# Loading v of later batches from GpSimd's queue, and spreading its block sums as one row

## The chip, the cores and the metric

The kernel runs on one core of a Trainium2 chip. The core has a matrix engine (TensorE, PE in the profile; its weight loads are PEld), a vector engine (VectorE, DVE), a scalar engine (ScalarE, ACT), GpSimd (POOL) and SyncE (SP). Each runs its own list of instructions in order and waits on semaphores. Transfers between memory and the on-chip buffers are issued from SP or from GpSimd, each with a queue of its own, and both queues are worked off by the same 16 DMA engines.

The metric is the time of one execution on the device, in microseconds, and it is judged against the kernel before.

## The reference

Four batches of 768 positions, 8 heads of 64, all fp32. For every batch an attention with a short window and with block summaries, then a gate that chooses one expert of eight for the whole batch, and that expert's two-layer network:

```python
k_sum = k.reshape(B, H, nb, block, D).max(axis=3)      # block = 32, nb = 24
v_sum = v.reshape(B, H, nb, block, D).mean(axis=3)
mask_l = np.abs(pos[:, None] - pos[None, :]) < window  # window = 16
scores_s = scale * einsum(q, k_sum) + np.log(block)
a = softmax(concat([where(mask_l, scale * q @ k.T, -1e9), scores_s]))
attn = a @ concat([v, v_sum])
...
pooled = x.mean(axis=1)                                # x: attn, heads side by side, 768 x 512
logits = pooled @ w_gate
e = argmax(logits);  gate_w = softmax(logits)[e]
out = gate_w * (relu(x @ w1[e]) @ w2[e])               # w1[e] 512 x 1024, w2[e] 1024 x 512
```

The output is 4 x 768 x 512 in fp32. Which expert's weights are loaded is known only when the attention of that batch is done.

## The kernel before

**The work of one batch.** q and k are loaded with a cast to bf16 by GpSimd's queue (`load_qk`, L197), in halves of four heads. For each of four pairs of heads TensorE transposes k and q (`tk` L403, `tq` L427), VectorE (in batch 0 ScalarE) copies k out into windows of 96 positions (`ek`, L425/L423), takes the block maxima (`km`, L445), and ScalarE spreads them (`kb`, L455). Two halves per pair follow: scores (`qk`, L463), exponential on ScalarE (L474), mask on VectorE (L478), the product with v (`av`, L496, called AV below), normalisation on VectorE (`nm`, L509 and L510), and once per pair the transpose of the result (`tx` L520, `xc` L528).

v is loaded in fp32 from SP's queue, one issue per head, with rows of 64 elements, that is 256 bytes (`load_v`, L209), into the one buffer `v_f`. VectorE casts it in four steps of two heads into `vblk` (L295), of which there are two that alternate by batch. `halo_v` (L297) copies the overlap of the windows from partition to partition. Then `v_ops` (L326) makes the block sums: `vs` multiplies with the 0/1 matrix `bind` (L355), `ev` copies the sums out (L367, `vsb`), and `bc` (L372) spreads them by DMA into rows 96 to 119 of `vblk`, once for each of the 12 query blocks. AV reads those rows, so it waits for `bc`.

The gate (`gate`, L625): logits on TensorE (L633), the maximum and its index on VectorE (L643 to L648), then GpSimd reads the index into a register and issues the loads of w1 and w2 of that expert with a cast to bf16 (L664, L670). The expert's network (`moe`, L712, "MoE 0" to "MoE 3" below): first layer L725 with ReLU on ScalarE (L740), second layer L759 with scaling (L769), and stores on SP (L772). The weights have two buffers, as have q and k.

**What sets the order.** The code that looks like a program only adds operations with an engine, an estimated duration, dependencies and "after" (issue order alone) to a planner, `Sched` (L22). At the end `run` (L67) plays these estimates through, engine by engine, prefers what has the longest tail of work behind it, and emits the instructions in that order. So each engine's list is fixed when the kernel is built. A transfer's end is estimated in L120 to L125: it starts 0.8 us after its issue or when its queue is free, takes `dma`, is lengthened by what the other queue still has to do (up to its own length), and is seen 1.2 us later. Where a transfer comes later than planned, everything behind the waiting instruction in that engine's list waits too.

The accumulator tile `ops` in PSUM has one buffer that `vs`, AV and the gate share in the order in which they are added. The loop at L794 adds attention of batch b, the gate of b, `v_ops` of b+1 and the MoE of b; so the block sums of b+1 come after the gate of b.

**The order of the loads before.** On GpSimd's queue: q and k of batch 0, first half of q and k of batch 1 (L801), w(0), second half of batch 1 (L817), first half of batch 2, w(1), second half of batch 2, first half of batch 3, w(2), second half of batch 3, w(3). On SP's queue, beside these: v(0), v(1), then v(2) after w(0) has been issued and the sums of batch 1 have left (`vl`, L807), then v(3) likewise.

Of the kernel before, what the change touches and what calls it, by code (L numbers as in the profile page):

```python
# [21 lines left out]
class Sched:  # L22
# [3 lines left out]
    URGENT = 3.0  # L26

# [39 lines left out]
    def run(self, t0):  # L67
# [28 lines left out]
        for _ in self.ops:  # L96
# [38 lines left out]
def kernel(  # L135
# [16 lines left out]
    QB = 64  # L152
# [38 lines left out]
    ]  # L191
    kts = [const_pool.tile([128, NJ, 128], BF16, name=f"kT{i}") for i in range(3)]
# [16 lines left out]
    def load_v(b, h):  # L209
        if b > 0:  # L210
            nc.sync.dma_start(v_f[16:80, :, h, :], v[b, h].rearrange("(j p) d -> p j d", p=QB))  # L211
            return
# [113 lines left out]
    def v_ops(b, loads):  # L326
# [17 lines left out]
        for gs in groups:  # L344
# [4 lines left out]
            st = {}  # L349

            def vs(b=b, gs=gs, st=st):
                ps = ops_pool.tile([128, 512], FP32, name="ops")
                for j in range(NJ):
                    for i, hg in enumerate(gs):
                        nc.tensor.matmul(  # L355
                            ps[32 * i : 32 * i + 32, 0 : HW * (D + 1)],
                            lhsT=bind[:, j, :],
                            rhs=vblks[b % 2][0:80, j, hg * HW : (hg + 1) * HW, :],
                            start=(j == 0),
                            stop=(j == NJ - 1),  # L360
                        )
                st["ps"] = ps

            def ev(b=b, gs=gs, st=st):
                n = 32 * len(gs)
                st["sb"] = sm_pool.tile([64, HW, D + 1], BF16, name="vsb")
                nc.vector.tensor_copy(  # L367
                    st["sb"][0:n],
                    st["ps"][0:n, 0 : HW * (D + 1)].rearrange("p (h c) -> p h c", c=D + 1),
                )  # L370

            def bc(b=b, gs=gs, st=st):  # L372
                for i, hg in enumerate(gs):
                    nc.sync.dma_start(
                        vblks[b % 2][KW:NR, :, hg * HW : (hg + 1) * HW, :],
                        st["sb"][32 * i : 32 * i + NB].unsqueeze(1).to_broadcast([NB, NJ, HW, D + 1]),
                    )
# [247 lines left out]
    def gate(b, x_ops, w_deps):  # L625
# [72 lines left out]
        o_ld = add("POOL", 1.5, [o_mx] + w_deps, ldf)  # L698
# [92 lines left out]
    casts, bcs = v_ops(0, v_loads)  # L791
    moe_last = {}
    w_order = []
    for b in range(B):  # L794
# [3 lines left out]
        sch.prio = 0.0  # L798
# [12 lines left out]
        sequence()  # L811
        w = gate(b, x_ops, moe_last.get(b - 2, []))
        w_order = [w[2]]
        sch.prio = 0.0
        if nxt < B:
            casts, bcs = v_ops(nxt, vl)
            qk_loads[nxt, 2] = qk_loads[nxt, 3] = add(  # L817
                "POOL", 1.3, prev, lambda n=nxt: load_qk(n, 4, 8), dma=4.7,
                after=[w[2], qk_loads[nxt, 0]],
            )  # L820
# [34 lines left out]
```

## Time and profile before

| | us |
|---|---|
| median of 3 runs | 229.79 (228.34 to 229.96) |
| the profiled execution's own time | 229.69 |
| its span in the profile | 228.1 |
| PE busy | 163.5 (72%) |
| VectorE busy | 100.9 (44%) |
| ScalarE busy | 96.9 (42%) |
| GpSimd busy | 24.6 (11%) |
| GpSimd's queue, packets' share of the 16 DMA engines | 13264 packets, 14.68 MB, 40.3% |
| SP's queue, likewise | 33584 packets, 15.47 MB, 32.2% |

The terms of the prediction are made against 229.69, the execution whose rows are read; it is 0.1 under the median, and 1.6 of it lie around the span.

How the views are read. The first page cuts the span into 40 slices of 5.7 us; a digit is the busy share in tenths. PEclk is TensorE's granted clock in tenths of full speed. A row in the order of time has the start, the duration, engine and line, operation, what it writes and reads, how many, and in brackets the idle time of that engine before it with what ended it. A row of the waits names who waited for whom, with the total, the number and the longest. The chain of waits starts from the last instruction and goes back, at each step, to what released it. The stretches give the busy time of each engine, the granted clock, the DMA engines' busy share (over 1 where packets of two queues overlap) and GB/s. "SPq" is the issuing of transfers on SP; a long SPq row is an issue that was held up.

### The profile page before, as it was taken

To read this page: it belongs to the slowest core of one execution; us is meant where nothing else is said; L and a number is where in the kernel's file an instruction comes from. 1 tells how busy PE (TensorE), PEld (TensorE's weight loads), DVE (VectorE), ACT (ScalarE), POOL (GpSimd) and SP (SyncE) were. 2 spreads that over 40 slices of the span, in tenths; PEclk is the share of its full clock that TensorE was granted. 3 is DMA by queue.
4 is the path that set the end of the run, shared out by engine and by line. 5 is a ranking of instruction groups with operands and counts; after the bars stand their busy time and mean duration, and the time that the engine had idled before them with its cause. 6 is when DMAs were issued, how large, how long until landed. Compare 5 with 4: busy or idle time off the path is not lost.

```text
span 228.1 us, 4604 instructions
## 1 busy us (share of the span) xinstructions
PE 163.5 (72%) x1938; PEld 97.3 (43%) x1960; DVE 100.9 (44%) x207; ACT 96.9 (42%) x182; POOL 24.6 (11%) x43
## 2 busy tenths in 40 slices
PE   0266797478770598993890588994998999089992
PEld 0244675354440465551450455542455544045540
DVE  5364788961302978740302969501269611000000
ACT  2121675334431265553140266623467954025532
POOL 7226000340000000240000000220000002000000
PEclk9999999999995559998598579999799999659998
DMA  6999994299999604399999703199970016990033
GB/s 105 206 183 166 213 174 84 32 165 171 207 197 192 80 3 73 89 156 222 200 196 179 204 0 67 50 166 237 252 139 3 3 50 151 251 194 3 0 152 124
DMA packets 46870, 30.45 MB, mean 133 GB/s; under 512 B 28225, under 2 KB 42145, under 8 KB 46753
## 3 DMA queue, kind: packets, MB, share of 16 engines
q0 software_dynamic: 13264, 14.68, 40.3%
q1 hardware_dynamic: 33584, 15.47, 32.2%
q8 instruction: 15, 0.25, 0.5%
q14 instruction: 7, 0.05, 0.1%
HBM read 36.06 MB, written 6.29 MB: 186 GB/s over the span
## 4 chain that ended last, share of the span: by engine, by line
PE 36%; DMA 28%; SPq 15%; DVE 10%; ACT 5%; issue 3%; POOL 1%; POOLq 1%; ACTq 0%; DVEq 0%
DMA v_f<-in_v_dram 15%; PE hps L725 11%; DMA q_nat<-in_q_dram 9%; SPq L211 9%; PE hps L759 8%; DMA w_sb<-in_moe_w_dram 5%; SPq L214 4%; PE ops L355 3%; PE tps L520 3%; PE tps L431 3%; DVE kT L425 3%; PE kps L406 3%; DVE vblk L295 2%; PE sc L463 2%; PE ops L496 2%
## 5 line engine op out<-in xcount | busy, mean ns | idle before, releaser
L725 PE MATMUL hps<-xT_b,w_sb 128*128 128x256 bf16 (+1 forms) x242 | 55.2, 371 | 14.3 <-DMA w_sb<-in_moe_w_dram 12.6
L740 ACT ACTIVATE hT_sb<-hps 128x512 bf16<-128x512 f32 (+1 forms) x64 | 29.8, 489 | 38.2 <-PE hps L725 36.8
L759 PE MATMUL hps<-w_sb,hT_sb 128*128 128x512 bf16 x184 | 43.2, 380 | 0.6 <-issue 0.3
L725 PEld LDWEIGHTS <-w_sb 128*128 128x128 bf16 x256 | 24.7, 108 | 30.3 <-DMA w_sb<-in_moe_w_dram 12.5
L474 ACT ACTIVATE aT<-sc 128x768 bf16<-128x768 f32 x32 | 25.9, 809 | 14.9 <-PE sc L463 14.6
L406 PE MATMUL kps<-identb,k_nat 96*64 96x96 bf16 x256 | 11.3, 249 | 25.5 <-DVE kT L425 18.0
L478 DVE TENSOR_TENSOR aT<-aT,mask 120x768 bf16<-120x768 bf16 x32 | 17.7, 556 | 23.0 <-ACT aT L474 22.9
L295 DVE CAST vblk<-v_f 80x1536 bf16<-80x1536 f32 x16 | 15.2, 956 | 26.4 <-DMA v_f<-in_v_dram 26.4
L759 PEld LDWEIGHTS <-hT_sb 128*128 128x128 bf16 x192 | 17.8, 98 | 19.8 <-issue 0.2
L769 ACT ACTIVATE o_sb<-hps,gcol 128x512 f32<-128x512 f32 x24 | 16.5, 686 | 22.4 <-PE hps L759 15.4
L528 ACT ACTIVATE xT_b<-tps 128x768 bf16<-128x768 bf16 x16 | 13.0, 810 | 27.4 <-PE tps L520 27.4
L406 PEld LDWEIGHTS <-k_nat 96*64 96x64 bf16 x256 | 9.4, 139 | 28.0 <-issue 20.6
L664 POOL DMA_DIRECT2D w_sb<-in_moe_w_dram x5 | 3.8, 757 | 156.9 <-DVE grec L684 116.8
L496 PE MATMUL ops<-vblk,aT 120*64 120x65 bf16 x384 | 14.4, 220 | 7.2 <-DMA vblk<-vsb 4.1
L510 DVE TENSOR_TENSOR xs<-ops,rv 128x384 bf16<-128x384 f32 x32 | 17.8, 557 | 1.1
L496 PEld LDWEIGHTS <-aT 120*64 120x64 bf16 x384 | 10.8, 130 | 16.4 <-DVE xs L510 4.7
L425 DVE COPY kT<-kps 128x1152 bf16<-128x1152 bf16 x12 | 16.1, 1346 | 0.5 <-PE kps L406 0.5
L463 PE MATMUL sc<-qT,kT 64*128 64x64 bf16 x384 | 13.8, 215 | 3.0 <-ACT aT L474 1.6
L445 DVE TENSOR_REDUCE kmx<-kT 128x24 bf16<-128x768 bf16 x16 | 15.1, 942 | 0.1
L355 PE MATMUL ops<-vblk,bind 80*32 80x260 bf16 x96 | 11.3, 348 | 5.1 <-DVE vblk L295 5.1
L463 PEld LDWEIGHTS <-kT 64*128 64x128 bf16 x384 | 9.7, 109 | 10.6 <-issue 7.1
L509 DVE RECIPROCAL rv<-ops 128x6 f32<-128x6 f32 x32 | 6.1, 191 | 15.7 <-PE ops L496 15.6
(53 smaller groups left out, 110.6 us busy)
## 6 DMA issues: line engine op xcount, KB each, us to landing
w_sb<-in_moe_w_dram POOLq DMA_DIRECT2D x7, 1024.0 KB, 14.8
out_dram<-o_sb SPq DMA_DIRECT2D x24, 256.0 KB, 2.0
v_f<-in_v_dram SPq DMA_DIRECT2D x24, 192.0 KB, 8.5
k_nat<-in_k_dram POOLq DMA_DIRECT2D x6, 384.0 KB, 19.4
q_nat<-in_q_dram POOLq DMA_DIRECT2D x6, 384.0 KB, 20.9
v_f<-in_v_dram SPq DMA_DIRECT2D x7, 240.0 KB, 6.7
vblk<-vsb SPq DMA_DIRECT2D x8, 146.2 KB
vblk<-vblk SPq DMA_DIRECT2D x6, 178.8 KB, 3.8
```

The source lines that it names most:

```text
L211: nc.sync.dma_start(v_f[16:80, :, h, :], v[b, h].rearrange("(j p) d -> p j d", p=QB))
L295: eng.tensor_copy(dst, v_f[:, :, hs, :])
L355: nc.tensor.matmul(ps[32 * i : 32 * i + 32, 0 : HW * (D + 1)], lhsT=bind[:, j, :], rhs=vblks[b % 2][0:80, j, hg * HW : (hg + 1) * HW, :], ...
L406: nc.tensor.transpose(kps[hh * D : (hh + 1) * D, g, 2 : 2 + SP], qk_nat[b][1][:, 2 * pr + hh, g, :], identb[0:SP, 0:SP],)
L425: nc.vector.tensor_copy(kdst, win)
L463: nc.tensor.matmul(sc[:, hh, jj * QB : (jj + 1) * QB], lhsT=sb["kT"][pr][rs, j, :], rhs=sb["qT"][pr][rs, j, :], start=True, stop=True, til ...
L474: nc.scalar.activation(aT, sb["sc"][:, :, 0 : NH * QB], ACT.Exp, scale=SCALE)
L496: nc.tensor.matmul(ops[(j % 2) * QB : (j % 2 + 1) * QB, hh, jj // 2, :], lhsT=aT[0:NR, hh, jj * QB : (jj + 1) * QB], rhs=vb[0:NR, j, 2 * p ...
L510: nc.vector.tensor_tensor(out=sb["xs"][pr][:, hf * NS : (hf + 1) * NS, :, :].rearrange("p s h d -> p h s d"), in0=ops[:, :, :, 0:D], in1=r ...
L725: nc.tensor.matmul(sb["hps"][:, 0 : c1 - c0], lhsT=sb["w1"][:, dt, ft * 128 : (ft + 1) * 128], rhs=sb["xT"][:, dt, c0:c1], start=(dt == 0) ...
L740: nc.scalar.activation(sb["hT"][:, ft, c0:c1], ps["t"][:, 0 : c1 - c0], ACT.Relu)
L759: nc.tensor.matmul(ps["t"], lhsT=sb["hT"][:, ft, st * 128 : (st + 1) * 128], rhs=sb["w2"][:, ft, :], start=(ft == 0), stop=(ft == NFT - 1),)
```

## The change

Five things are changed.

1. `load_v` of batches 1 to 3 issues from GpSimd's queue instead of SP's, still in fp32 and by head.
2. A new function `load_next` adds the loads of one batch as one file: first half of q and k, eight loads of v, second half of q and k. For batch 1 it is called before the gate of batch 0, and the gate's load is ordered after it (`order`). For batch n+1 beyond that it is called when `v_ops` of batch n has been added, ordered after the second weight load of the batch before. So GpSimd's queue holds: batch 0; batch 1; w(0); batch 2; w(1); batch 3; w(2); w(3).
3. The block sums of a later batch are 12 matmuls of 8 heads x 64 columns into one set of 32 partitions, instead of 24 matmuls of 4 heads x 65 columns into two sets. The column of the constant 32, which came out of the matmul, is filled once into two fixed tiles `vsbs`.
4. The spread of a later batch is one issue with rows of 8 heads x 65 bf16 elements, 1040 bytes, instead of two with rows of 520 bytes.
5. The planner's estimates are changed: the lengthening by the other queue is 0.3 of a transfer's own length on GpSimd's queue and up to twice its own length on SP's, and the landing is seen 1.3 us later.

```diff
+    SHARE = {"POOL": 0.3, "SP": 2.0}
...
-                shared = min(op["dma"], max(0.0, other - begin))
+                shared = min(self.SHARE[eng] * op["dma"], max(0.0, other - begin))
                 rings[eng] = begin + op["dma"] + shared
-                op["end"] = rings[eng] + 1.2
+                op["end"] = rings[eng] + 1.3
...
+    vsbs = [const_pool.tile([NB, H, D + 1], BF16, name=f"vsb{i}") for i in range(2)]
...
     def load_v(b, h):
         if b > 0:
-            nc.sync.dma_start(v_f[16:80, :, h, :], v[b, h].rearrange("(j p) d -> p j d", p=QB))
+            nc.gpsimd.dma_start(v_f[16:80, :, h, :], v[b, h].rearrange("(j p) d -> p j d", p=QB))
...
+        for t in vsbs:
+            nc.vector.memset(t[:, :, D : D + 1], float(BLK))
...
                 for j in range(NJ):
-                    for i, hg in enumerate(gs):
-                        nc.tensor.matmul(
-                            ps[32 * i : 32 * i + 32, 0 : HW * (D + 1)],
-                            lhsT=bind[:, j, :],
-                            rhs=vblks[b % 2][0:80, j, hg * HW : (hg + 1) * HW, :],
...
+                    nc.tensor.matmul(
+                        ps[0:32, 0 : n * D],
+                        lhsT=bind[:, j, :],
+                        rhs=vblks[b % 2][0:80, j, hs, 0:D],
...
                 nc.vector.tensor_copy(
-                    st["sb"][0:n],
-                    st["ps"][0:n, 0 : HW * (D + 1)].rearrange("p (h c) -> p h c", c=D + 1),
+                    vsbs[b % 2][:, hs, 0:D],
+                    st["ps"][0:NB, 0 : n * D].rearrange("p (h c) -> p h c", c=D),
                 )
...
-                for i, hg in enumerate(gs):
-                    nc.sync.dma_start(
-                        vblks[b % 2][KW:NR, :, hg * HW : (hg + 1) * HW, :],
-                        st["sb"][32 * i : 32 * i + NB].unsqueeze(1).to_broadcast([NB, NJ, HW, D + 1]),
-                    )
+                nc.sync.dma_start(
+                    vblks[b % 2][KW:NR, :, hs, :],
+                    vsbs[b % 2][:, hs, :].unsqueeze(1).to_broadcast([NB, NJ, n, D + 1]),
+                )
...
-            o_ev = add("DVE", 0.42, [o_vs], ev)
+            o_ev = add("DVE", 0.06 + 0.27 * len(gs), [o_vs, dve_setup] + prev, ev)
...
-            o_bc = add("SP", 0.6 * len(gs), [o_ev], bc, dma=0.8 * len(gs))
+            o_bc = add("SP", 0.5, [o_ev], bc, dma=1.0 * len(gs))
...
-        o_ld = add("POOL", 1.5, [o_mx] + w_deps, ldf)
+        o_ld = add("POOL", 1.5, [o_mx] + w_deps, ldf, after=order)
...
+    def load_next(n, prev, casts, order):
+        sch.prio = 0.0
+        qk_loads[n, 0] = qk_loads[n, 1] = add(
+            "POOL", 1.3, prev, lambda: load_qk(n, 0, 4), dma=4.8, after=order
+        )
+        vl = []
+        for h in range(H):
+            vl.append(
+                add(
+                    "POOL", 0.9, casts, lambda h=h: load_v(n, h), dma=0.95,
+                    after=vl[-1:] or [qk_loads[n, 0]],
+                )
+            )
+        qk_loads[n, 2] = qk_loads[n, 3] = add(
+            "POOL", 1.3, prev, lambda: load_qk(n, 4, 8), dma=4.8, after=vl[-1:]
+        )
+        order_pool[:] = [qk_loads[n, 2]]
+        return vl
...
-        if nxt < B:
-            prev = last_T.get(nxt - 2, [])
-            qk_loads[nxt, 0] = qk_loads[nxt, 1] = add(
-                "POOL", 1.3, prev, lambda n=nxt: load_qk(n, 0, 4), dma=4.7, after=order_pool
-            )
-            vl = []
-            for h in range(H):
-                vl.append(
-                    add("SP", 0.6, casts, lambda n=nxt, h=h: load_v(n, h), dma=0.87, after=vl[-1:] + bcs + w_order)
-                )
...
         sequence()
-        w = gate(b, x_ops, moe_last.get(b - 2, []))
-        w_order = [w[2]]
+        prev = last_T.get(nxt - 2, [])
+        if b == 0:
+            vl = load_next(nxt, prev, casts, order_pool)
+        w = gate(b, x_ops, moe_last.get(b - 2, []), order_pool)
         sch.prio = 0.0
         if nxt < B:
             casts, bcs = v_ops(nxt, vl)
-            qk_loads[nxt, 2] = qk_loads[nxt, 3] = add(
-                "POOL", 1.3, prev, lambda n=nxt: load_qk(n, 4, 8), dma=4.7,
-                after=[w[2], qk_loads[nxt, 0]],
-            )
-            order_pool = [qk_loads[nxt, 2]]
+        if nxt + 1 < B:
+            vl = load_next(nxt + 1, last_T[b], casts, [w[2]])
         moe_last[b] = moe(b, w, xsl)
```

More of the change, by code (lines that the diff above doesn't have):

```diff
@@ L362, in vs, with ev @@
                 st["ps"] = ps
-            def ev(b=b, gs=gs, st=st):
-                n = 32 * len(gs)
-                st["sb"] = sm_pool.tile([64, HW, D + 1], BF16, name="vsb")
+            def ev(b=b, n=n, hs=hs, st=st):
                 nc.vector.tensor_copy(
-                    st["sb"][0:n],
-                    st["ps"][0:n, 0 : HW * (D + 1)].rearrange("p (h c) -> p h c", c=D + 1),
-                )
-            def bc(b=b, gs=gs, st=st):
-                for i, hg in enumerate(gs):
-                    nc.sync.dma_start(
-                        vblks[b % 2][KW:NR, :, hg * HW : (hg + 1) * HW, :],
-                        st["sb"][32 * i : 32 * i + NB].unsqueeze(1).to_broadcast([NB, NJ, HW, D + 1]),
-                    )
+                    vsbs[b % 2][:, hs, 0:D],
+                    st["ps"][0:NB, 0 : n * D].rearrange("p (h c) -> p h c", c=D),
+                )
@@ L623, in attention, with gate @@
         return sequence, xsl, x_ops
-    def gate(b, x_ops, w_deps):
+    def gate(b, x_ops, w_deps, order):
         sb = state[b]
@@ L791 @@
     casts, bcs = v_ops(0, v_loads)
+    def load_next(n, prev, casts, order):
[13 more added lines that the diff above has]
+            "POOL", 1.3, prev, lambda: load_qk(n, 4, 8), dma=4.8, after=vl[-1:]
+        )
+        order_pool[:] = [qk_loads[n, 2]]
+        return vl
     moe_last = {}
-    w_order = []
     for b in range(B):
```

10 lines of the change are left out of this document (5 added, 5 removed).

## The prediction

> **What bounds the kernel now.** I read the first page, then the list of waits, the chain of waits, and the busy times by stretch. The page's slices:
>
> ```profile
> span 228.1 us, 4604 instructions
> PE   0266797478770598993890588994998999089992
> PEclk9999999999995559998598579999799999659998
> DMA  6999994299999604399999703199970016990033
> ```
>
> Each slice is 5.7 us, counted from 0. Neither TensorE nor the transfers are busy throughout; they alternate. TensorE stands or halves in slices 12, 18, 21, 27 and 34, and its granted clock sinks in and behind most of these holes, while the transfers run near nine tenths before them and stand at 14, 23, 30 and 36. So no engine is the bound: a loop through both is. The waits name it (us in total, times, longest), and SP's row in the order of time and the chain of waits show it for batch 1 (start, us, what):
>
> ```profile
> DVE vblk L295 <- DMA v_f<-in_v_dram: 26.4, 8, 8.7
> ```
> ```profile
> 51.89 22.19 SPq L211 DMA_DIRECT2D v_f<-in_v_dram  x8
> ```
> ```profile
> 61.65 12.57 DMA v_f<-in_v_dram
> 74.31 0.96 DVE vblk L295
> 75.27 1.28 DVE kT L425
> 76.59 0.85 PE kps L406 x16
> ```
>
> TensorE needs kT of batch 1 at 68.5. VectorE could make it, but its program has the cast of batch 2's v ahead of it, and that v lands at 74. The eight issues of v stand on SP from 51.89 to 74.08, because their packets share the engines with the weights, k and q issued shortly before on GpSimd's queue. Stretches (us, then busy time of PE, PEld, DVE, ACT, POOL, clock, DMA share, GB/s):
>
> ```profile
> 68.50:76.60 8.10, 0.01 (x2) 0.01 (x3) 3.91 (x6) 0.60 (x1) 0.00 (x0) 0.56 1.22 181
> 76.60:95.30 18.70, 17.40 (x240) 11.04 (x243) 15.78 (x30) 10.51 (x22) 0.00 (x0) 0.73 0.22 50
> 104.60:108.70 4.10, 0.00 (x0) 0.00 (x0) 0.00 (x0) 0.69 (x1) 0.00 (x0) 0.79 1.18 204
> 119.40:128.00 8.60, 0.01 (x1) 0.11 (x1) 3.89 (x6) 0.60 (x1) 0.00 (x0) 0.77 1.02 196
> 128.00:146.80 18.80, 17.09 (x233) 10.89 (x235) 15.53 (x29) 11.84 (x26) 0.03 (x1) 0.83 0.20 51
> 156.70:160.00 3.30, 0.00 (x1) 0.00 (x0) 0.56 (x1) 1.39 (x2) 0.00 (x0) 1.00 1.19 221
> 160.00:193.40 33.40, 32.25 (x400) 17.59 (x406) 15.96 (x36) 20.80 (x41) 1.64 (x2) 0.95 0.44 96
> 193.40:200.20 6.80, 0.00 (x0) 0.00 (x0) 0.16 (x1) 0.44 (x1) 0.00 (x0) 0.67 1.11 251
> 200.20:228.10 27.90, 23.63 (x110) 11.79 (x112) 0.00 (x0) 11.32 (x22) 0.00 (x0) 0.87 0.35 91
> ```
>
> Five holes of TensorE: 8.1, 4.1, 8.6, 3.3 and 6.8 us, 30.9 in all. Where data is there (160 to 193) it is 97% busy.
>
> **The change, part by part.** The sum is made against this execution: span 228.1, its own time 229.69 (1.6 around the span), the median of the runs 229.79.
>
> *Order and queue of the loads.* Today batch 1's second half of q and k is issued behind batch 0's weights, and v(2) on SP beside them. Rows in the order of time show what comes when:
>
> ```profile
> 43.35 1.50 POOL L664 DMA_DIRECT2D w_sb<-in_moe_w_dram  x2 [22.81 <-DVE grec L684]
> 45.71 0.72 POOL L204 DMA_DIRECT2D k_nat<-in_k_dram  x1
> 66.97 0.53 PE L431 MATMUL tps<-identb,q_nat 96*64 96x96 bf16 x16 [1.12 <-DMA q_nat<-in_q_dram]
> 41.81 0.94 DVE L295 CAST vblk<-v_f 80x1536 bf16<-80x1536 f32 x1
> ```
>
> After: q, k (both halves) and v of batch 1 stand in one file ahead of w(0), then w(0), qk(2), v(2), w(1), qk(3), v(3), w(2), w(3). The slices show the transfers idle (4, then 2) from 34 to 45, so the second half of batch 1 fits before w(0) at 43.35. Attention 1 then has all its q and k at 43, not at 67. v(2) still lands at about 71 to 74, as the same bytes go out behind w(0), but VectorE's list can now put attention 1 ahead of that cast, since nothing of it is missing. So the holes at 68.5 and 119.4 go: -16.7. Behind them the clock was 0.73 and 0.83; at full clock the busy 17.40 and 17.09 would shrink by up to 4.7 and 2.9, but VectorE has 15.8 and 15.5 in these stretches, so I take half: -3.8.
>
> *What the move adds.* GpSimd gets 24 issues, 8 per batch, at 0.72 (the row at 45.71) 5.8 us, beside transfers of 8: hidden. v(2) waits there for the last cast of v(1), with qk(2)'s second half and gate 1's load behind it; that cast ends at 42.75 and v(2)'s turn is near 49, so 0 (if the cast were 10 us later, 4). SP loses 24 issues, and stores no longer queue behind them. Two small fills on VectorE lie in the first 7 us, ahead of the first v: 0.
>
> The transfer's own price on GpSimd's queue is not in the trace. The nearest rows, from 8 to 10 us (SP alone, rows of v) and from 190 to 206 (w(3)):
>
> ```profile
> DMA packets 1577, 0.40 MB, mean 199 GB/s; under 512 B 1577, under 2 KB 1577, under 8 KB 1577
> q0 software_dynamic: 1568, 2.10, 80.0%
> ```
>
> One batch of v is 8*768 = 6144 packets of 256 B. At the first row 6144/1577*2 = 7.8 us. If a packet kept the second row's price (0.80 of 16 engines for 16 us, over 1568 packets, is 0.13 us) it would be 6144*0.13/16 = 50 us. I take 7.8, as only the first row has this packet size, and keep the other for a rival.
>
> An issue on GpSimd beside a cast on VectorE is in the trace once:
>
> ```profile
> 17.90 1.30 POOL L204 DMA_DIRECT2D q_nat<-in_q_dram  x1
> 18.10 0.96 DVE L295 CAST vblk<-v_f 80x1536 bf16<-80x1536 f32 x1 [2.43 <-DMA v_f<-in_v_dram]
> ```
>
> It took 1.30 instead of about 0.7. At four casts a batch that is 2.4 us at most, behind transfers already queued: 0. The Trainium skill (SBUF — State Buffer, the "DVE blocks DMA" trap in its section on the two separate sides) says that VectorE's copies in a two-port mode lock GpSimd out of the port through which it writes descriptors, and advises the hardware queue. That speaks against this move; the 1.30 agrees with it. By that rule, with all of it on the path, the sum below would be 3*2.4 = 7 us higher; by the row it is 0.
>
> *Block sums.* The sums become 12 matmuls of 512 columns instead of 24 of 260, then a wider copy, then one issue instead of two, with half the packets. The rows in the order of time (start, us, what, idle time before), and one of the chain for 8 matmuls of 512 columns:
>
> ```profile
> 46.81 2.79 PE L355 MATMUL ops<-vblk,bind 80*32 80x260 bf16 x24
> 52.35 1.49 PE L725 MATMUL hps<-xT_b,w_sb 128*128 128x512 bf16 x3 [2.32 <-DMA w_sb<-in_moe_w_dram]
> 59.33 0.38 PE L496 MATMUL ops<-vblk,aT 120*64 120x65 bf16 x12 [0.84 <-issue]
> 96.29 1.51 PE L355 MATMUL ops<-vblk,bind 80*32 80x260 bf16 x24
> 98.28 1.75 SPq L374 DMA_DIRECT2D vblk<-vsb  x2
> 108.73 0.54 PE L496 MATMUL ops<-vblk,aT 120*64 120x65 bf16 x12 [4.13 <-DMA vblk<-vsb]
> 49.64 0.42 DVE L367 CAST vsb<-ops 64x260 bf16<-64x260 f32 x1 [0.84 <-PE ops L355]
> ```
> ```profile
> 91.44 1.73 PE hps L759 x8
> ```
>
> At full clock 12*1.73/8 = 2.6 against 1.51: +1.1 for batches 2 and 3. At the low clock of batch 1, 12*1.49/3 = 6.0 against 2.79: +3.2. The copy reads 512 columns instead of 260: between 0.42 and 0.83, +0.3. From the end of the second issue (100.03) to the matmul is 8.7 us. Half the packets in turn with the weights' make 4.3 if the taking of turns sets it, 8.7 if not. I take 4.3, and one issue less is -0.9. So logits to first AV is 3.8 us shorter in batch 2 (4.3+0.9-1.1-0.3) and 1.7 in batch 1, where it ran to 59.33. The hole of 4.1 goes (-4.1), TensorE gets 5.4 us of work (+5.4); without the halving the hole stays and the part costs about 5.
>
> *The end.* The rows of the gates' logits (L633) and of the first AV (L496), in the order of time:
>
> ```profile
> 40.99 0.20 PE L633 MATMUL ops<-wg_sb,pooled 128*1 128x8 f32 x2 [0.76 <-ACT xT_b L528]
> 93.10 0.34 PE L633 MATMUL ops<-wg_sb,pooled 128*1 128x8 f32 x8
> 164.63 0.54 PE L496 MATMUL ops<-vblk,aT 120*64 120x65 bf16 x12
> 187.43 0.35 PE L633 MATMUL ops<-wg_sb,pooled 128*1 128x8 f32 x8
> 200.26 13.38 PE L725 MATMUL hps<-xT_b,w_sb 128*128 128x512 bf16 x63 [6.90 <-DMA w_sb<-in_moe_w_dram]
> ```
>
> From one gate's logits to the next: logits to first AV was 15.6 (93.10 to 108.73), after the change 11.8; first AV to next logits is 22.8 (164.63 to 187.43), with MoE work in between. So 34.6 a turn; batch 1's turn takes 52.1 today (40.99 to 93.10).
>
> Gate 0 at 41; batch 1's own cold sums make its first step 16.6 (59.3-41.0-1.7), so gate 1 at 41+16.6+22.8 = 80, gates 2 and 3 at 115 and 150 instead of 187. Most of MoE 2 (as much work as MoE 3, 23.6) is then still undone and covers the 12.8 us from the last logits to MoE 3's first matmul: holes of 3.3 and 6.8 go, -10.1, and MoE 3 runs warm: its first 64 matmuls, half of 512 and half of 256 columns, took 13.4; at 1.73 for 8 of 512 they would take 10.4, -3.0.
>
> Sum: 229.7 - 16.7 - 3.8 - 4.1 + 5.4 - 10.1 - 3.0 = 197.4. What is late next: weights, k, q and v of a batch keep the transfers busy from 44 to about 78 (slices 8 to 13, the last at 6), 34 us, as long as the new turn of 34.6. So a turn has no slack, and I put back a wait for a transfer of 3.3 (the row at 156.7) in each of two turns: +6.6. **204.**
>
> **The rivals.**
> *B. A wait takes the place of the old.* The lists of the engines are fixed by planned landings; w(1) is now behind qk(2) and v(2), w(2) behind qk(3) and v(3), stores beside them. If one cast or weight is late in each of two turns by what v costs today (8.1 and 8.6 in place of the 6.6), that is 197.4 + 16.7 = 214. For it: today's plan was wrong by just that. Against: batch 1's loads are early.
>
> *C. Slower: v's short packets are dear on GpSimd's queue.* With e us more per batch, v(1) costs e-5 (the idle before 43), and v(2) and v(3) e each. w(0) at 43.4, two turns of 34, less the half of qk(3) behind v (5), landing to first AV 11.8, attention 22.8, logits to MoE 3 12.8, from there to the end 27.9 (the last stretch) and 1.6: 43.4+68-5+11.8+22.8+12.8+27.9+1.6+3e-5 = 178.3+3e, which passes 229.7 at e = 17, a v of 25 us. At e = 20 it is 238. For it: the 50 us end. Against: the same engines took these packets in 0.02 us each.
>
> *D. It does nothing.* The bytes are the same, so v ends when it did and the casts block as before; only the sums change: 229.7 - 4.1 + 5.4 = 231. The Trainium skill (DMA: Bandwidth & Descriptors, "Issuing engines are not separate DMA queues") says that the issuing engine saves issue time alone, which would give this. The trace speaks against it in one point: q at 66.97 is late by its place behind w(0), and the place is what changes.
>
> *E. All holes go and no new one comes:* 197, or less with more of the cold clock gone.
>
> **How the numbers follow.** Forecast 0.54, B 0.24, C 0.08, D 0.06, E 0.08. The predicted time is the forecast's, 204. The range reaches from E to past B: 195 to 218. It leaves out C, D and the edges, 0.2. A measurement here can tell about 1% from no change. Faster by over 1%: forecast, B, E, 0.86; within 1%: D, 0.06; slower: C, 0.08.
>
> **What would show it.** Right: k, q and v of batch 1 landed by 43; no hole of TensorE near 68 and 119; logits of gates 1 to 3 near 80, 115, 150; clock near full from 60 on; no hole before MoE 3. The wait on the spread sums is under a microsecond, or its landing about 4 us after issue. Wrong: rows of v on GpSimd's queue that take far over 8 us a batch (C); VectorE again idle 8 us before a cast of v, or TensorE before weights (B); gates where they were (D).

## The result, and the profile after

The changed kernel takes 200.25 us, the median of four runs (198.33 to 207.69), against 229.38 for the kernel before beside it (228.34 to 229.96): a ratio of 0.867, 95% interval 0.860 to 0.874. Some executions of a kernel are slower than its others at no change of the program, and all ratios here are formed without them, so that they differ a little from the quotient of the medians. The execution whose rows follow took 201.35, with a span of 199.8.

The first page after, with its slices now of 5.0 us:

```profile
span 199.8 us, 4547 instructions
PE 160.0 (80%) x1902; PEld 93.0 (47%) x1924; DVE 100.7 (50%) x209; ACT 95.7 (48%) x182; POOL 42.4 (21%) x67
PE   0342877765989799999999899958999995399992
PEclk9999999999999999999999999996999999579999
```

From slice 14 on TensorE no longer alternates with the transfers: it is at eight or nine tenths up to the last slice, except for two places (slices 26 and 33 to 34), and the clock sinks only in and behind these (slices 27, 34 and 35). The stretches (columns as before) give these two holes and what lies around them:

```profile
59.00:77.50 18.50, 16.23 (x252) 10.04 (x254) 14.10 (x29) 12.91 (x27) 3.61 (x5) 1.00 1.16 195
77.50:121.70 44.20, 42.63 (x488) 22.95 (x498) 26.39 (x50) 25.47 (x51) 10.32 (x14) 1.00 1.00 188
133.00:135.40 2.40, 0.00 (x0) 0.11 (x2) 2.15 (x4) 0.34 (x1) 0.00 (x0) 1.00 1.11 180
135.40:167.50 32.10, 31.77 (x384) 17.13 (x388) 15.41 (x35) 20.34 (x41) 1.65 (x2) 0.95 0.35 78
167.50:172.90 5.40, 0.00 (x1) 0.00 (x0) 0.16 (x1) 0.69 (x1) 0.00 (x0) 0.76 1.09 243
```

From 77.5 to 121.7 TensorE works 96% of the time (42.63 of 44.20) while the transfers are also busy throughout (DMA share 1.00). Before, these two kinds of time followed each other.

The waits after (us in total, times, longest):

```profile
POOL v_f L213 <- DMA w_sb<-in_moe_w_dram: 26.0, 4, 8.3
PE hps L726 <- DMA w_sb<-in_moe_w_dram: 7.9, 2, 5.4
DVE vblk L299 <- DMA v_f<-in_v_dram: 7.7, 4, 3.5
```

VectorE waits 7.7 us for v instead of 26.4. GpSimd now stands 26.0 us before issues of v while weights go out; experiment 5 shows what that costs. TensorE's two holes are both waits for weights.

TensorE in the order of time: the gates' logits (L634), the sums (L359), the first AV of each batch (L497) and the end:

```profile
43.78 0.20 PE L634 MATMUL ops<-wg_sb,pooled 128*1 128x8 f32 x2 [0.76 <-ACT xT_b L529]
49.60 5.30 PE L359 MATMUL ops<-vblk,bind 80*32 80x512 bf16 x12
64.76 0.38 PE L497 MATMUL ops<-vblk,aT 120*64 120x65 bf16 x12
77.47 0.20 PE L634 MATMUL ops<-wg_sb,pooled 128*1 128x8 f32 x2 [0.42 <-ACT xT_b L529]
85.90 2.80 PE L359 MATMUL ops<-vblk,bind 80*32 80x512 bf16 x12
99.45 0.38 PE L497 MATMUL ops<-vblk,aT 120*64 120x65 bf16 x12
121.68 0.35 PE L634 MATMUL ops<-wg_sb,pooled 128*1 128x8 f32 x8
142.18 0.38 PE L497 MATMUL ops<-vblk,aT 120*64 120x65 bf16 x12
159.83 0.35 PE L634 MATMUL ops<-wg_sb,pooled 128*1 128x8 f32 x8
160.11 7.08 PE L760 MATMUL hps<-w_sb,hT_sb 128*128 128x512 bf16 x32
172.93 0.61 PE L726 MATMUL hps<-xT_b,w_sb 128*128 128x512 bf16 x1 [5.43 <-DMA w_sb<-in_moe_w_dram]
173.75 11.83 PE L726 MATMUL hps<-xT_b,w_sb 128*128 128x512 bf16 x61 [0.22 <-issue]
```

The gates' logits stand at 43.8, 77.5, 121.7 and 159.8. In batches 1 to 3 the first AV no longer waits for the spread sums: none of the three rows of L497 has idle time before it. (In batch 0 one AV still waits 1.4 us for them.) Behind the last logits only 32 matmuls of MoE 2 are left, 7.1 us; then TensorE stands 5.4 us until w(3) has landed.

### The profile page after: what moved, and what is told of

It reads as the page before. It is cut to its first block, busy times and chain, and to the rows that moved or that the text cites. A ratio compares the mean times of both kernels' runs of the same rounds, so it can differ in the third digit from the quotient of the medians.

```text
span 199.8 us, 4547 instructions
## 1 busy us (share of the span) xinstructions
PE 160.0 (80%) x1902; PEld 93.0 (47%) x1924; DVE 100.7 (50%) x209; ACT 95.7 (48%) x182; POOL 42.4 (21%) x67
## 4 chain that ended last, share of the span: by engine, by line
PE 55%; DMA 25%; DVE 6%; SPq 4%; issue 3%; ACT 3%; POOL 2%; POOLq 1%; ACTq 0%
PE hps L726 23%; PE hps L760 15%; DMA w_sb<-in_moe_w_dram 11%; DMA v_f<-in_v_dram 7%; DMA q_nat<-in_q_dram 4%; PE ops L359 4%; PE sc L464 4%; SPq L216 3%; PE ops L497 3%; DMA vblk<-vblk 2%; PE kps L407 2%; PE tps L521 2%; PE tps L432 2%; DVE kT L426 1%; DVE xs L511 1%
## 5 line engine op out<-in xcount | busy, mean ns | idle before, releaser
L726 PE MATMUL hps<-xT_b,w_sb 128*128 128x256 bf16 (+1 forms) x239 | 50.3, 343 | 9.3 <-DMA w_sb<-in_moe_w_dram 7.9
L741 ACT ACTIVATE hT_sb<-hps 128x512 bf16<-128x512 f32 x64 | 29.8, 490 | 23.4 <-PE hps L726 22.5
L726 PEld LDWEIGHTS <-w_sb 128*128 128x128 bf16 x256 | 23.3, 102 | 24.1 <-DMA w_sb<-in_moe_w_dram 7.9
L760 PEld LDWEIGHTS <-hT_sb 128*128 128x128 bf16 x192 | 18.0, 98 | 20.5 <-issue 0.9
L213 POOL DMA_DIRECT2D v_f<-in_v_dram x24 | 18.0, 761 | 36.4 <-DMA w_sb<-in_moe_w_dram 26.0
L359 PE MATMUL ops<-vblk,bind 80*32 80x512 bf16 (+1 forms) x60 | 16.3, 445 | 6.0 <-DVE vblk L299 6.0
L479 DVE TENSOR_TENSOR aT<-aT,mask 120x768 bf16<-120x768 bf16 x32 | 17.6, 552 | 4.6 <-ACT aT L475 4.4
L497 PE MATMUL ops<-vblk,aT 120*64 120x65 bf16 x384 | 13.7, 211 | 4.9 <-DVE xs L511 2.0
L529 ACT ACTIVATE xT_b<-tps 128x768 bf16<-128x768 bf16 x16 | 12.9, 809 | 8.9 <-PE tps L521 8.8
L497 PEld LDWEIGHTS <-aT 120*64 120x64 bf16 x384 | 10.0, 122 | 12.9 <-issue 5.0
L464 PE MATMUL sc<-qT,kT 64*128 64x64 bf16 x384 | 13.1, 210 | 2.9 <-ACT kT L456 1.2
L407 PEld LDWEIGHTS <-k_nat 96*64 96x64 bf16 x256 | 9.2, 139 | 10.6 <-DMA k_nat<-in_k_dram 7.2
L464 PEld LDWEIGHTS <-kT 64*128 64x128 bf16 x384 | 9.2, 105 | 10.0 <-issue 6.4
## 6 DMA issues: line engine op xcount, KB each, us to landing
w_sb<-in_moe_w_dram POOLq DMA_DIRECT2D x7, 1024.0 KB, 15.8
```

The costliest lines, as they stand in the source:

```text
L213: nc.gpsimd.dma_start(v_f[16:80, :, h, :], v[b, h].rearrange("(j p) d -> p j d", p=QB))
L359: nc.tensor.matmul(ps[0:32, 0 : n * D], lhsT=bind[:, j, :], rhs=vblks[b % 2][0:80, j, hs, 0:D], start=(j == 0), stop=(j == NJ - 1),)
L407: nc.tensor.transpose(kps[hh * D : (hh + 1) * D, g, 2 : 2 + SP], qk_nat[b][1][:, 2 * pr + hh, g, :], identb[0:SP, 0:SP],)
L464: nc.tensor.matmul(sc[:, hh, jj * QB : (jj + 1) * QB], lhsT=sb["kT"][pr][rs, j, :], rhs=sb["qT"][pr][rs, j, :], start=True, stop=True, til ...
L479: nc.vector.tensor_tensor(out=aT[0:NR], in0=aT[0:NR], in1=mask[:, hf * NH : (hf + 1) * NH, :] .rearrange("p j c -> p (j c)") .unsqueeze(1) ...
L497: nc.tensor.matmul(ops[(j % 2) * QB : (j % 2 + 1) * QB, hh, jj // 2, :], lhsT=aT[0:NR, hh, jj * QB : (jj + 1) * QB], rhs=vb[0:NR, j, 2 * p ...
```

## The experiments

Medians in us and ratios to the kernel before on the same chip (229.44, 229.02 and 229.87 in the three groups of runs), with a 95% interval; where there were too few runs for an interval, the ratio is left out:

| | in the expectations | kernel | us | ratio |
|---|---|---|---|---|
| 1 | e4 | before, lists remade for v on GpSimd, v issued on GpSimd | 214.44 | |
| 2 | e6 | the lists of 1, v issued on SP as before | 211.42 | 0.925 (0.913 to 0.936) |
| 3 | e1 | after, v on SP, planned there | 212.45 | 0.927 (0.911 to 0.943) |
| 4 | e5 | after, v on SP, lists kept | 234.25 | 1.028 (1.016 to 1.040) |
| 5 | e10 | after, v on SP behind the spread, lists kept | 202.05 | 0.878 (0.871 to 0.885) |
| 6 | e2 | after, old sums | 204.00 | 0.895 (0.884 to 0.906) |
| 7 | e3 | after, old planner's constants | 204.58 | 0.894 (0.879 to 0.908) |
| 8 | e8 | after, attention preferred | 217.22 | |
| 9 | e7 | after, last w1 halved in the plan | 204.50 | |
| 10 | e9 | after again | 202.13 | 0.879 (0.871 to 0.886) |
| 11 | e11 | after, last w1 as two issues, lists kept | 194.81 | |
| 12 | e12 | 11 with v(1) on SP | 194.39 | 0.850 (0.843 to 0.857) |

**1. The queue and its lists, nothing else.** The kernel before, with v on GpSimd's queue at its old place in the order of loads; old sums, old planner's constants.

```diff
-            nc.sync.dma_start(v_f[16:80, :, h, :], v[b, h].rearrange("(j p) d -> p j d", p=QB))
+            nc.gpsimd.dma_start(v_f[16:80, :, h, :], v[b, h].rearrange("(j p) d -> p j d", p=QB))
...
-                    add("SP", 0.6, casts, lambda n=nxt, h=h: load_v(n, h), dma=0.87, after=vl[-1:] + bcs + w_order)
+                    add("POOL", 0.9, casts, lambda n=nxt, h=h: load_v(n, h), dma=0.95, after=vl[-1:] + bcs + w_order)
```

> The kernel before (229.4 us) with one part of the change: v of batches 1 to 3 is issued from GpSimd's queue, but at its old place in the order, so behind w(0), the second half of q and k of batch 1 and the first half of batch 2. Theory 'place': q and k of batch 1 are as late as before (67 us) and v(2) ends at about 74, so the holes stay: 222 to 232. Rival 'queue': without two queues sharing the engines the holes go: 208 to 216.

Measured: 214.44 (212.46 to 217.16). Half of the gain is there although q and k of batch 1 are as late as before. But this edit changes two things, the queue and, through the planner, the lists of all engines.

**2. The lists of 1 without the queue.** The second line of that diff stays, so the planner makes the same lists; the first is taken back, so v goes out from SP.

> The kernel before (229.4 us) with the lists of TensorE, VectorE and ScalarE that the queue alone gave (214.4 us: all four casts of the next v stand behind two copies of kT), but v issued from SP as before. Theory 'lists': most of the 15 us that the queue alone gave came from the place of the casts in VectorE's list, so 213 to 219, and TensorE has no hole of 8 us at 68 and 119. Rival 'queue': the 15 us came from v no longer sharing the engines; with v on SP again 224 to 231.

Measured: 211.42 (208.98 to 212.08), 17.6 under the kernel before in the same group, and not slower than 1. So moving the queue gained nothing here; the lists did. SP's row of v(2), then VectorE around the old hole, first in this kernel:

```profile
51.39 22.16 SPq L211 DMA_DIRECT2D v_f<-in_v_dram  x8
```
```profile
64.97 1.36 DVE L425 COPY kT<-kps 128x1152 bf16<-128x1152 bf16 x1 [1.52 <-PE kps L406]
68.66 1.36 DVE L425 COPY kT<-kps 128x1152 bf16<-128x1152 bf16 x1
73.06 0.95 DVE L295 CAST vblk<-v_f 80x1536 bf16<-80x1536 f32 x1
```

and then in the kernel before:

```profile
71.81 0.96 DVE L295 CAST vblk<-v_f 80x1536 bf16<-80x1536 f32 x1 [8.72 <-DMA v_f<-in_v_dram]
74.31 0.96 DVE L295 CAST vblk<-v_f 80x1536 bf16<-80x1536 f32 x1 [0.85 <-DMA v_f<-in_v_dram]
75.19 1.35 DVE L425 COPY kT<-kps 128x1152 bf16<-128x1152 bf16 x1
77.78 1.34 DVE L425 COPY kT<-kps 128x1152 bf16<-128x1152 bf16 x1
```

The transfer of v(2) is as slow as it was (22.16 against 22.19 of issuing). What differs is the order on VectorE: the kernel before has two casts of v(2) ahead of the two copies of kT, and the copies wait for v until 75; here the copies run at 65 and 69, and the casts come behind them, without idle time before them. TensorE's wait of 8.1 us for kT is gone with that: the longest of its waits between 55 and 90 us is 1.62. Two smaller holes stay in this kernel, 3.2 us for the spread sums at 97.8 and 4.0 us for k at 148.7. The lists differ in other places too, on TensorE among them, so the 17.6 is the worth of the new lists, of which this place is the one that the waits show.

**3. v planned on SP.** The changed kernel with its order of loads, but v of batches 1 to 3 planned on and issued from SP, behind the spread of the batch before.

```diff
-            nc.gpsimd.dma_start(v_f[16:80, :, h, :], v[b, h].rearrange("(j p) d -> p j d", p=QB))
+            nc.sync.dma_start(v_f[16:80, :, h, :], v[b, h].rearrange("(j p) d -> p j d", p=QB))
...
-                    "POOL", 0.9, casts, lambda h=h: load_v(n, h), dma=0.95,
-                    after=vl[-1:] or [qk_loads[n, 0]],
+                    "SP", 0.6, casts, lambda h=h: load_v(n, h), dma=0.87,
+                    after=vl[-1:] or [qk_loads[n, 0]] + bcs,
```

> The changed kernel (200.2 us) with one part undone: v of batches 1 to 3 is issued from SP again, at the new place in the order (after the first half of q and k of the same batch, and after the spread sums of the batch before). Theory 'place': what removed the holes is that q, k and v of a batch stand a batch earlier and that the cast of v stands behind the attention in VectorE's list; the queue itself matters little: 199 to 206, no hole of 8 us before a cast, w(b) landing up to 8 us later because v shares the engines with it. Rival 'queue': one file is what counts; with two queues v lands late again and a hole of about 8 us comes back in each of two turns: 212 to 218.

Measured: 212.45 (210.90 to 214.27). SP in the order of time, and ScalarE's step that follows from it:

```profile
90.56 15.75 SPq L213 DMA_DIRECT2D v_f<-in_v_dram  x5
106.42 2.25 SPq L773 DMA_DIRECT2D out_dram<-o_sb  x1
```
```profile
113.38 0.69 ACT L770 ACTIVATE o_sb<-hps,gcol 128x512 f32<-128x512 f32 x1 [9.06 <-DMA out_dram<-o_sb]
```

Five issues of v hold SP for 15.8 us; a store stands behind them, its buffer is not free, and ScalarE waits 9.06 us for it. This run alone does not tell the queue from the lists, as both changed.

**4. v on SP, lists kept.** Only the first line of that diff; the planner still thinks that v is on GpSimd, so the orders of the compute engines stay.

> The changed kernel (200.2 us) with v of batches 1 to 3 issued from SP, while the lists of TensorE, VectorE and ScalarE stay exactly those of the changed kernel; on SP five of the eight issues of v(2) stand ahead of the spread of batch 1. Theory 'lists': the queue is not what counts but where the casts stand; 200 to 204, no hole before a cast of v. Rival 'queue': v on a second queue slows the weights, k and q, and the spread behind it on SP comes late: a hole of 3 to 8 us before the first AV of batch 1 or before MoE 0, w(b) landing later, 207 to 214.

Measured: 234.25 (232.62 to 235.23), slower than the kernel before. SP, then TensorE:

```profile
43.77 17.63 SPq L213 DMA_DIRECT2D v_f<-in_v_dram  x5
61.50 3.79 SPq L375 DMA_DIRECT2D vblk<-vsb  x1
```
```profile
75.42 0.54 PE L497 MATMUL ops<-vblk,aT 120*64 120x65 bf16 x12 [13.29 <-DMA vblk<-vsb]
```

Five of the eight issues of v(2) stand on SP ahead of the spread of batch 1. They are held up for 17.6 us while w(0) goes out, so the spread leaves at 61.5 to 65.3 instead of at once, and the first AV of batch 1 waits 13.3 us. Stores are caught in the same way: ScalarE waits 29.3 us in all for them in this kernel, against 8.2 in the changed one.

**5. v on SP behind the spread, lists kept.** As 4, but the issues of v(n) are held back until the spread of batch n-1 has been issued.

```diff
+            issue = lambda: nc.sync.dma_start(v_f[16:80, :, h, :], v[b, h].rearrange("(j p) d -> p j d", p=QB))
+            held.append(issue) if b - 1 not in spread else issue()
...
+                if hs.stop == H:
+                    spread.add(b)
+                    while held:
+                        held.pop(0)()
```

> The changed kernel with v of batches 1 to 3 issued from SP and the lists of TensorE, VectorE and ScalarE kept, but on SP the loads of a later v stand behind the spread of the batch before (in the run with the lists kept before, five stood ahead of it). Theory 'SP is held': v on SP hurts because spread and stores of SP stand behind its issues, which are held up while the weights go out; with the spread ahead the wait of 13 us before the first AV of batch 1 goes, the stores' waits stay: 210 to 222. Rival 'shared engines': the time is lost because v and the weights share the engines, wherever v stands on SP: 228 or more. Rival 'lists alone': 199 to 205.

Measured: 202.05 (200.04 to 204.46), beside 202.13 for the changed kernel in the same group (run 10). SP:

```profile
55.47 0.87 SPq L378 DMA_DIRECT2D vblk<-vsb  x1
56.39 19.86 SPq L215 DMA_DIRECT2D v_f<-in_v_dram  x8
```

With the spread ahead of them, the eight issues may take 19.9 us and nobody misses SP. So with these lists v on GpSimd's queue is worth nothing that can be seen; its use is that nothing urgent stands behind it there. The 26.0 us for which GpSimd stands in the changed kernel do not show in the time either: in this kernel that wait does not exist, and the time is the same. (It has more waits of another kind, 15.4 us of ScalarE for stores against 8.5 in run 10, so the two kernels are equal in sum, not in every part.)

**6. The old sums in the changed kernel** (24 matmuls of 260 columns, the old copy, two issues and their old estimates; the lines with a minus in the diff of the change).

> The changed kernel with the block sums of the kernel before: 24 matmuls of 260 columns in two sets, two issues with rows of 520 bytes. Theory 'sums are hidden': in the changed kernel no AV of batches 1 to 3 waits for the spread rows, so the old form costs nothing on the path and gives TensorE some 5 us of work back: 196 to 201. Rival 'sums are on the path', as the prediction had it: the spread lands 4 us later in each batch, AV waits up to 4 us: 203 to 210.

Measured: 204.00 (203.29 to 205.01), against 200.25 and 202.13 for the changed kernel in other groups. The lists change with the estimates, and TensorE has a wait for the halo here:

```profile
88.35 2.57 PE L359 MATMUL ops<-vblk,bind 80*32 80x260 bf16 x22 [4.88 <-DMA vblk<-vblk]
```

Runs 9 and 11 show such a wait at the same place with the new sums (3.14 us in run 9), so it does not belong to the old ones. The new sums are worth between nothing and some 4 us; the runs do not say it more closely.

**7. The old planner's constants.**

```diff
-                shared = min(self.SHARE[eng] * op["dma"], max(0.0, other - begin))
+                shared = min(op["dma"], max(0.0, other - begin))
...
-                op["end"] = rings[eng] + 1.3
+                op["end"] = rings[eng] + 1.2
```

> The changed kernel with the planner's old estimate of a transfer (lengthened by the other queue up to its own length on both queues, seen 1.2 us later). Theory 'place': the order of the loads is written out and stays, so 199 to 204. Rival 'estimates': the new estimates are what put the casts of v behind the attention in VectorE's list; with the old ones a cast stands too early again and a hole of 4 to 8 us comes back: 206 to 216.

Measured: 204.58 (202.77 to 206.06). The new constants bring between nothing and some 4 us; the holes before MoE 2 and 3 are there as after (2.7 and 5.3).

**8. Attention preferred.** The planner's preference for attention and gate, which batch 0 has, for all batches.

```diff
-        sch.prio = 40.0 if b == 0 else 0.0
+        sch.prio = 40.0
```

> The changed kernel with the planner's priority of batch 0's attention and gate given to those of all batches, so that attention stands ahead of MoE work in the lists. Theory 'lists filled with MoE work make the gates late': gates 1 to 3 come earlier by 5 us or more, MoE 2 is left to cover the load of w(3), the hole of 5.4 before MoE 3 goes: 194 to 198. Rival: attention alone can't fill TensorE, as its steps wait for VectorE and ScalarE in turn; holes of 1 to 2 us appear between its steps and the time is 202 or more.

Measured: 217.22 (212.78 to 219.51). The casts of v kept their low preference and slid back: those of v(1) ran at 54.6 in one file of four instead of 40.6 to 45.5, and with them the halo, the sums and gate 1 (logits at 96.5). So the run does not test whether earlier gates with the same casts would pay; it shows casts in another late place, in a kernel that takes some 13 to 17 us more than the changed one. In this run five issues of v on GpSimd come beside these casts (VectorE, then GpSimd):

```profile
54.64 3.56 DVE L299 CAST vblk<-v_f 80x1536 bf16<-80x1536 f32 x4
55.89 5.62 POOL L213 DMA_DIRECT2D v_f<-in_v_dram  x5 [5.80 <-DVE vblk L299]
```

The first of the five took 2.67 us, from 55.89 to 58.56, and the casts ended at 58.20; the others took about 0.75 each.

**9. The last w1 halved in the plan.** Batch 3's first weights as two loads, as batch 0's are, so that MoE 3 can begin on the first half.

```diff
-            fs = slice(half * (F // 2), (half + 1) * (F // 2)) if b == 0 else slice(0, F)
+            fs = slice(half * (F // 2), (half + 1) * (F // 2)) if b in (0, B - 1) else slice(0, F)
...
-        if b == 0:
+        if b in (0, B - 1):
```

> The changed kernel with w1 of batch 3 loaded in two halves, as batch 0's is, so that MoE 3 can start on the first half. Theory 'last hole': the 5.4 us before MoE 3 wait for the whole of w1; the first half lands 2 to 4 us earlier: 196 to 198.5. Rival: the halves land together, since the queue works on both: 199 to 201.

Measured: 204.50 (199.94 to 208.07). The hole before MoE 3 shrank from 5.4 to 3.0 and its first layer ran in 10.57, but the lists changed elsewhere: there is a new hole of 3.1 for the halo before the sums of batch 2, and the one before MoE 2 is 3.3 instead of 2.5. Inconclusive, hence run 11.

**10. The changed kernel again,** in the group of 5, 11 and 12.

> The changed kernel itself once more, beside the next three: every theory expects 198 to 202, and holes of TensorE of about 2.5 us before MoE 2 and 5.4 us before MoE 3.

Measured: 202.13 (199.29 to 209.69), 0.9% from the first measurement. Its trace has the same two holes, 2.4 us before MoE 2 and 5.2 before MoE 3.

**11. The last w1 as two issues, lists kept.** One step of the planner issues two halves.

```diff
-            nc.gpsimd.dma_start(
-                sb["w1"][:, :, fs],
+            parts = [slice(0, F // 2), slice(F // 2, F)] if b == B - 1 else [fs]
+            for fp in parts:
+                nc.gpsimd.dma_start(
+                    sb["w1"][:, :, fp],
```

> The changed kernel with w1 of batch 3 issued as two halves, within one step of the planner, so that all lists of compute stay as they are. Theory 'last hole': MoE 3 starts when the first half is there, the hole of 5.4 us shrinks to 2 to 3: 196 to 199, ratio 0.98 to 0.99 of the changed kernel. Rival: the halves land together: no difference.

Measured: 194.81 (190.22 to 200.76), 7.3 under run 10, without an interval. In its trace the hole before MoE 3 is 1.0 us and MoE 3's first layer takes 10.57.

**12. The same with v(1) on SP,** to bring gate 0 forward.

```diff
+            (nc.sync if b == 1 else nc.gpsimd).dma_start(v_f[16:80, :, h, :], v[b, h].rearrange("(j p) d -> p j d", p=QB))
```

> The one before with v of batch 1 alone issued from SP again, lists of compute kept. In the runs so far the logits of gate 0 came at 40.5 to 41 us where v(1) is on SP, and at 42.4 to 44 where it is on GpSimd's queue. Theory 'v(1) in GpSimd's queue delays batch 0' (its larger packets hold up the rows that SP spreads for batch 0): gate 0 back at 41, the whole 1.5 to 2.5 us shorter than without this edit. Rival: the later gate 0 is covered by what TensorE does behind it, no difference beyond 1 us.

Measured: 194.39 (193.28 to 200.00). Its interval, 0.843 to 0.857, lies below the changed kernel's in both of its measurements: a version that beats both kernels. Gate 0's logits come at 40.5 instead of 42.7 in run 11, but the time is run 11's, so v(1) on SP adds nothing that can be seen beside a spread of some 7 to 10 us between single runs. The end in run 10, then in this one:

```profile
161.27 0.35 PE L634 MATMUL ops<-wg_sb,pooled 128*1 128x8 f32 x8
174.15 0.61 PE L726 MATMUL hps<-xT_b,w_sb 128*128 128x512 bf16 x1 [5.20 <-DMA w_sb<-in_moe_w_dram]
174.97 11.31 PE L726 MATMUL hps<-xT_b,w_sb 128*128 128x512 bf16 x61 [0.22 <-issue]
```
```profile
158.11 0.34 PE L634 MATMUL ops<-wg_sb,pooled 128*1 128x8 f32 x8
167.02 10.57 PE L728 MATMUL hps<-xT_b,w_sb 128*128 128x512 bf16 x62 [1.24 <-DMA w_sb<-in_moe_w_dram]
```

From the last logits to MoE 3 it is 8.9 instead of 12.9 us, the hole is 1.2 instead of 5.2, and the first layer takes 10.6 instead of 12.1: 5.5 us. Another 3.2 lie ahead of the last logits. Together they are the 8.6 us between the two spans (200.5 and 191.9). The 5.5 come from the halves, as run 11 has the same end without v(1) on SP: 8.7, 1.0 and 10.6. Where the 3.2 come from is not shown: gate 0 is 1.1 earlier here than in run 10 (40.5 against 41.7), but the two traces of the changed kernel itself, that of the result and run 10, lie 3.4 apart at gate 1 (77.5 and 80.9).

## Why the prediction was right, step by step

The forecast was 204.0 with a range of 195 to 218; measured were 200.25 and 202.13. It was right in size, in part by luck: two of its larger terms were wrong and nearly offset each other, as the last points below show. The five holes of 30.9 us have become two of 7.9 (2.46 and 5.43): 23.0 gone, where 24.3 were forecast net of the 6.6 put back. The rest of the 28.3 us between the spans, 5.3, stands against a forecast of 1.4 (the cold clock's 3.8 and 3.0 less the sums' 5.4). The granted clock rose from 0.892 to 0.974 on average, and busy TensorE fell from 163.5 to 160.0 although the sums grew; the forecast had counted only half of what the clock could bring in two stretches.

- **The holes at 68.5 and 119.4** went as forecast. Why they go was half right. The text named VectorE's list, with casts ahead of attention, and said that the list could be put right since q and k of batch 1 come early. Run 2 has the list put right with q as late as before:

```profile
66.54 0.53 PE L431 MATMUL tps<-identb,q_nat 96*64 96x96 bf16 x16 [1.62 <-DMA q_nat<-in_q_dram]
```

  So the holes go without an early q and k; remade lists, in which the casts stand behind the copies, are enough. Putting q, k and v in one file ahead of the weights was worth a further 10, with the new constants and the old sums (run 1 to run 6: 214.4 to 204.0) and likewise with the old constants and the new sums (run 7: 204.6). So neither the new constants nor the new sums are needed for it; what the two runs share is the new order of the loads, with the lists that follow from it.

- **The transfer's own price on GpSimd's queue** was taken at the cheap end, 7.8 us a batch, with 50 kept for rival C. C is refuted. It counted 6144 packets of 256 bytes a batch; GpSimd's queue made 512 of them, of 3 KB each (worked out in the last section). Between 66 and 74 us, where three issues of v and a half of q and k go out, GpSimd's queue moves nearly all there is:

```profile
DMA packets 530, 1.46 MB, mean 182 GB/s; under 512 B 117, under 2 KB 199, under 8 KB 528
q0 software_dynamic: 528, 1.43, 104.7%
```

  That is close to the 199 GB/s of the row the forecast took, though not for v alone.

- **The wait of a GpSimd issue beside a cast** was given 0 by the row and 7 by the rule of the Trainium skill (SBUF — State Buffer, the "DVE blocks DMA" trap). The 24 issues of v took (least, median, most, in ns):

```profile
L213 POOL DMA_DIRECT2D v_f<-in_v_dram x24: 746/752/801, 21.2 to 107.1; - x24
```

  None was as long as the 1.30 us seen once before, and run 5, without any of them on GpSimd, was no faster. So the 0 was right for the time, but the rule was not put to the test: in this kernel no issue of v runs beside a cast of v. The issues run from 21 to 31, from 50 to 69 and from 83 to 108 us, the casts of v(1) to v(3) from 40.6 to 45.5, from 74.4 to 79.2 and from 112.6 to 118.4. Where they do meet, the delay is there: 2.67 us for one issue in run 8, and 1.29 for an issue of k at 19.3 here.

- **Rival D** (the queue does nothing) had the queue worth nothing and the casts blocking as before. On the queue it was right: runs 5 and 10 agree with the rule it drew on (the Trainium skill, DMA: Bandwidth & Descriptors, "Issuing engines are not separate DMA queues"): 202.05 from SP, 202.13 from GpSimd. On the time it was wrong, because the lists and the order of loads changed with the queue.

- **The sums** were sized well: 5.30 in batch 1 where 6.0 was forecast and 2.80 in batch 2 where it was 2.6. The hole of 4.1 before AV went. AV of batch 2 now starts 22 us after the logits, with work of MoE between, so there is other work beside the spread. Run 6, with the old sums and two issues, has no wait of AV in batches 1 to 3 either: the new order removes this hole, not the new sums. Whether half the packets land in half the time (the 4.3 us of the forecast) stays open, since nothing waits for them any more.

- **The chain of turns is the step that failed.** Gates 1 to 3 were forecast near 80, 115 and 150 and came at 77.5, 121.7 and 159.8. Logits to first AV was put at 11.8 and took 22.0 and 20.5 in batches 2 and 3 (99.45 less 77.47, 142.18 less 121.68). In batch 1 it was put at 16.6 and took 21.0 (64.76 less 43.78), and from there to the next logits it was 12.7 instead of 22.8, so that gate 1 came near its 80 by luck. The forecast took a turn as a chain of waits. From 77 to 167 it is TensorE's work that sets it, with the expert's matmuls put between by the lists: but for the hole of 2.5 at 133 it is 96 to 99% busy.

- **The end** did not go as forecast either. With gate 3 at 160 instead of 150, only 7.1 us of MoE 2 were left to cover the 13.1 from the last logits to MoE 3 (159.83 to 172.93). The hole stayed at 5.4 of 6.8, and MoE 3's first layer took 12.65 (172.93 to 185.58) instead of 13.4 before and the forecast 10.4. Of the 10.1 and 3.0 us that the forecast took off here, 2.2 and 0.7 came. The two errors work against each other. Before the put-back, the forecast had gate 3 at 150 and the end of the span at 195.8 (197.4 less 1.6), 45.8 between them; measured are 159.8 and 40.0, so 9.8 later and 5.8 shorter. Run 12 shows the end that was forecast, by another way: hole 1.2, first layer 10.6.

- **The 6.6 put back** for waits on transfers was near in size (7.9) but wrong in kind and place: it stood for new waits within the turns, and what is there is the rest of the two old holes before MoE 2 and MoE 3, which the sum had taken off. That it makes up for most of the miss at the end is luck.

What stays open is the share of the new sums, and how much of the 17.6 us of run 2 belongs to the two casts alone: no run moves only these and leaves the rest of the lists as they were.

## What to carry to other kernels

Where each engine's list is fixed beforehand, look at who is queued behind a wait before asking which queue is faster: with v on SP the kernel took 234 or 202 us by what stood behind these issues, and 202 with v on GpSimd's queue. A change that moves a load also remakes the lists through the planner; separate the two by building the old issue with the new lists, as run 2 did. At the end of a kernel, where no other work covers a load, let the first half of it land on its own: that was worth some 5.5 us in the traces here.

## What the runs showed of the hardware

The 256-byte rows of v travel in larger packets from GpSimd's queue. The queues of the changed kernel (packets, MB, share of the 16 engines):

```profile
q0 software_dynamic: 14800, 19.40, 59.6%
q1 hardware_dynamic: 13868, 10.75, 21.3%
```

GpSimd's queue has 1536 packets more than before, 64 for each of the 24 issues of 192 KB, so 3 KB each; SP's has 19716 fewer, of which 18432 are the rows of v (24 issues of 768). Issues of v are held up on either queue while weights go out: on GpSimd for 26.0 us in four waits, the longest 8.3, on SP for 16 to 24 us per batch in run 5.

Halo transfers land in 6.2 us instead of 3.8, and stores in 5.1 instead of 2.0. Run 5 has 6.4 and 5.0 with v on SP, so v's queue is not the cause. Run 3, with the new order of loads but other lists, has 3.9 and 5.9, and runs 1 and 2, with the old order, have 3.9 for the halo and 2.1 and 2.2 for the stores. So the stores are slower with the new order; why the halo is slower in some of these kernels stays open.
